# Gated decode attention on one core: V of a step and K of the next as one 8 MiB transfer

## The chip, the core and the metric

The kernel runs on one core of one Trainium2 chip. The metric is device time in microseconds (us) of one execution. TensorE (PE) multiplies matrices, VectorE (DVE) and ScalarE (ACT) work on elements, GpSimd (POOL) does almost nothing here, and SyncE (SP) issues the transfers from the chip's memory. Sixteen DMA engines carry the bytes of this core.

## The reference, cut to what matters

One token for each of two batch entries (B = 2, D = 448) attends to a cache of 4096 positions. There are 16 query heads and 8 key/value heads, each of width 256. All data is fp32. K and V of the cache are 64 MiB each, so that 128 MiB of the 158.54 MB of reads (1 MiB is 1.05 MB) are the cache; the rest is weights.

```python
xn = _layernorm(x)                                   # [2, 1, 448]
q  = (xn @ wq).reshape(B, 1, 16, 256)                # two query heads share one K/V head
scores = einsum("bhqd,bhkd->bhqk", q, k) * 256**-0.5
o  = einsum("bhqk,bhkd->bhqd", softmax(scores), v)
s  = o.reshape(B, 1, 4096) @ wo
h  = (xn @ w_gate) * (xn @ w_up)                     # bilinear GLU
g  = silu(h @ w_down)
return x + s * g
```

## The kernel before

**Steps.** One step is one pair of a K/V head and a batch entry, so there are N = 16 steps, `i` = 0 to 15. Its K and its V are 4 MiB each, laid out in memory as 128 rows of 32 KB, one row for each partition. `scores(i)` (matmuls at L205) multiplies K of the step with the query, `softmax` (L210 to L231) makes the probabilities, and `values(i)` (matmuls at L237) multiplies them with V. `scores` and `values` are 16 matmuls each, which fp32 turns into 32 in the profile. `softmax` is a chain through three engines: a maximum on DVE, a transpose on PE (L213) and a second maximum on DVE that leaves one value in each element of a row, a matmul with a one (L218) that brings this row back to a column, an exponential on ACT, a transpose on DVE, and a matmul (L229) that adds up the sums.

**Work between the steps.** `query(0)` and `query(1)` project the token to queries with `wq0` and `wq1`. `ffn_in` and `ffn_out` compute the gate from `wg`, `wu` and `wd`. `combine` (L246) and `turn` (L256) bring finished outputs into the form that the output projection needs, `project` (L264) does that projection with `wo0` (16 blocks) and `wo1` (8 blocks), `spread` (L167) adds its partial sums up, and `project_last` (L270) does the last 8 blocks, with `wo2`.

**Order.** The instructions of every engine run in the order in which the program writes them (`manual_schedule`). A step of the loop writes `scores(i)`, `softmax`, `values(i)`. After the loop over the first 14 steps come `combine` of 6 outputs, `turn`, `project` with `wo1`, `spread`, then `scores` and `softmax` of step 14, `scores` and `softmax` of step 15, `values(14)`, `values(15)` in two halves, and the small rest.

**Buffers.** All large reads go through one ring of five buffers of 32 KB for each partition. `plan` writes down the order of the reads, `issue` (transfers at L59, all on SP's queue) starts the next ones. SP waits, in order, until the buffer that a transfer needs is free; five transfers are issued before any work. The order is wq0, k0, v0, k1, v1, wg, wu, k2, v2, wd, k3, v3, and so on with one K and one V for each step; its end is k13, v13, wo1, k14, k15, v14, v15 (in three pieces), wo2 (in four pieces). wo1 and wo2 are 1.75 MiB each.

Of the kernel before, what the change touches and what calls it, by code (L numbers as in the profile page):

```python
# [25 lines left out]
EARLY = 16  # L26
LATE = 24
THIRD = [24, 25, 28, 29, 30, 31, 26, 27]
EPS = 1e-5


# [2 lines left out]


@with_exitstack
def gated_decode_block(ctx: ExitStack, tc: tile.TileContext, x, xo, kt, v, wq, wo, wg, wu, wd, out):
    nc = tc.nc
    ring = ctx.enter_context(tc.tile_pool(name="ring", bufs=5))
    const = ctx.enter_context(tc.tile_pool(name="const", bufs=1))  # L40
    work = ctx.enter_context(tc.tile_pool(name="work", bufs=2))
    psum = ctx.enter_context(tc.tile_pool(name="psum", bufs=1, space=bass.MemoryType.PSUM))
# [2 lines left out]
    def bank(name="s", bufs=3):  # L45
        return psum.tile([128, 512], F32, name=name, bufs=bufs)


    loaded = {}
    todo = []  # L50

    def plan(name, src, cuts=None):
        todo.append((name, src, cuts or [0, src.shape[1]]))

    def issue(n=1):
        for name, src, cuts in todo[:n]:
            t = loaded[name] = ring.tile([128, ROW], F32, name="ring", align_bytes=512)
            for lo, hi in zip(cuts, cuts[1:]):
                nc.sync.dma_start(t[:, lo:hi], src[:, lo:hi])  # L59
        del todo[:n]  # L60

    N = HKV * B
    LAST = N - B
    plan("wq0", wq[0])
    for i in range(LAST):
        if i == 2:
            plan("wg", wg)
            plan("wu", wu)
        if i == 3:
            plan("wd", wd)  # L70
        if i == 6:
            plan("wq1", wq[1])
        if i == 9:
            plan("wo0", wo[:, :EARLY * D])
        plan(f"k{i}", kt[i % B, i // B])
        plan(f"v{i}", v[i % B, i // B])
    plan("wo1", wo[:, EARLY * D:LATE * D])
    plan(f"k{LAST}", kt[0, HKV - 1])
    plan(f"k{LAST + 1}", kt[1, HKV - 1])
    plan(f"v{LAST}", v[0, HKV - 1])  # L80
    plan(f"v{LAST + 1}", v[1, HKV - 1], [0, 4096, 7168, 8192])
    plan("wo2", wo[:, LATE * D:], [0, 2 * D, 6 * D, 7 * D, 8 * D])
    issue(5)

    x2 = const.tile([B, D], F32)
    nc.scalar.dma_start(x2, x)
# [48 lines left out]
    def rows(ps, w, n):  # L135


        def block(i):
            return w[:, i * n:(i + 1) * n]

        for k in range(3):
            for c in range(NT):
                nc.tensor.matmul(ps[W * c:W * (c + 1), :n], xnT[:, k, :], block(NT * k + c), start=k == 0, stop=False)  # L143
        for c in range(NT):
            half = slice(0, 64) if c < 2 else slice(64, 128)
            nc.tensor.matmul(ps[W * c:W * (c + 1), :n], xnT[half, 3, :], block(12 + c % 2)[half], start=False, stop=True)  # L146
# [4 lines left out]
    def query(h):  # L151
        ps = bank()
        rows(ps, loaded[f"wq{h}"], 512)
        for r in range(REP):
            nc.vector.transpose(qT[h][:, :, :, :, r, :].rearrange("p b g d j -> p (g d) b j"),  # L155
                                ps[:, r * 256:(r + 1) * 256])
# [10 lines left out]
            nc.tensor.matmul(dst[W * n:W * (n + 1), :SL], add_tiles.rearrange("p b j -> p (b j)"),  # L167
                             t[:, n * SL:(n + 1) * SL], start=start, stop=stop)

    def ffn_in():  # L170
        pp = []
        for w in ("wg", "wu"):
            ps = bank()
            rows(ps, loaded[w], FC)
            pp.append(ps)
        g = work.tile([128, FC], F32, name="h")
        nc.scalar.copy(g, pp[0][:, :FC])
        h = work.tile([128, FC], F32, name="h")
        nc.vector.tensor_mul(h, pp[1][:, :FC], g)
        nc.vector.transpose(hT.rearrange("p i m -> p (i m)"), h)  # L180

    def ffn_out():
        ps = bank()
        for i in range(14):
            t = i % NT
            nc.tensor.matmul(ps[W * t:W * (t + 1), :D], hT[:, i], loaded["wd"][:, i * D:(i + 1) * D],  # L186
                             start=i < NT, stop=i >= 14 - NT)
        y = bank()
        spread(ps, y, True, True)
        e = const.tile([128, SL], F32)  # L190
        nc.scalar.activation(e, y[:, :SL], AF.Sigmoid)
        nc.vector.tensor_mul(gate, y[:, :SL], e)


    def scores(i):
        g, b = divmod(i, B)
        k = loaded[f"k{i}"].rearrange("p (h d c n) -> p h d c n", h=2, d=2, c=NT)
        q = qT[g // 4][:, b, g % 4].rearrange("p d r j -> p d (r j)")
        m = work.tile([128, 4], F32, name="m")
        ss = []  # L200
        for h in range(2):
            s = bank()
            for d in range(2):
                for c in range(NT):
                    nc.tensor.matmul(s[W * c:W * (c + 1), :], q[:, d], k[:, h, d, c, :], start=d == 0, stop=d == 1)  # L205
            nc.vector.tensor_reduce(m[:, h:h + 1], s, axis=AX.X, op=OP.max)  # L206
            ss.append(s)
        return ss, m

    def softmax(ss, m):  # L210
        nc.vector.tensor_max(m[:, 2:3], m[:, 0:1], m[:, 1:2])  # L211
        sm = bank("sm", 1)
        nc.tensor.transpose(sm[:1, :128], m[:, 2:3], ident)  # L213
        mx = work.tile([1, NT, W], F32, name="mx")
        nc.vector.tensor_reduce(  # L215
            mx, sm[:1, None, :128].rearrange("p o (c j) -> p o j c", c=NT).to_broadcast([1, NT, W, NT]),
            axis=AX.X, op=OP.max)
        nc.tensor.matmul(sm[:, 128:129], mx.rearrange("p c j -> p (c j)"), one, start=True, stop=True)  # L218
        nc.vector.tensor_scalar(m[:, 3:4], sm[:, 128:129], -1.0 / 16, None, op0=OP.mult)  # L219
        su = work.tile([128, 4], F32, name="su")  # L220
        pT = []
        for h in range(2):
            p = work.tile([128, 512], F32, name="p")
            nc.scalar.activation(p, ss[h], AF.Exp, bias=m[:, 3:4], scale=1.0 / 16, accum_out=su[:, h:h + 1])  # L224
            t = work.tile([128, KB, W], F32, name="pT", bufs=4)
            nc.vector.transpose(t.rearrange("p i m -> p (i m)"), p)  # L226
            pT.append(t)
        nc.vector.tensor_add(su[:, 2:3], su[:, 0:1], su[:, 1:2])  # L228
        nc.tensor.matmul(sm[:, 130:131], add_head.rearrange("p a r j -> p (a r j)"), su[:, 2:3], start=True, stop=True)  # L229
        nc.vector.reciprocal(su[:, 3:4], sm[:, 130:131])  # L230
        return pT, su[:, 3:4]  # L231

    def values(i, pT, o, lo=0, hi=KB):

        for e in range(lo, hi):
            h, t, at = e // 8, e % NT, e % 8 * 2 * W
            nc.tensor.matmul(o[W * t:W * (t + 1), :], pT[h].rearrange("p i m -> p (i m)")[:, at:at + 2 * W:2],  # L237
                             loaded[f"v{i}"][:, e * 512:(e + 1) * 512], start=e < NT, stop=e >= KB - NT)
# [22 lines left out]
    def project(oT, first, lo, hi, name, base):  # L261
        for i in range(lo, hi):
            t = i % NT
            nc.tensor.matmul(wide[W * t:W * (t + 1), :D], heads(oT, i, first),  # L264
                             loaded[name][:, (i - base) * D:(i - base + 1) * D], start=i < NT, stop=i >= LATE - NT)
# [5 lines left out]
                             start=False, stop=i == THIRD[-1])  # L271

    query(0)
    issue()
    ob = work.tile([128, 8, 512], F32, name="ob", bufs=1)
    oT0 = const.tile([128, 4, 2, REP, W], F32)
    oT1 = const.tile([128, 3, 2, REP, W], F32)
    oT2 = const.tile([128, 1, 2, REP, W], F32)
    for i in range(LAST):
        g, b = divmod(i, B)  # L280
        ss = scores(i)
        issue()
        p = softmax(*ss)
        o = bank("o", 1)
        values(i, p[0], o)
        nc.scalar.activation(ob[:, b * 4 + g if g < 4 else b * 3 + g - 4], o, AF.Copy, scale=p[1])  # L286
        issue()
        if i == 1:
            ffn_in()
            issue(2)  # L290
        if i == 2:
            ffn_out()
            issue()
        if i == 5:
            query(1)
            issue()
        if i == 7:
            cb = combine(ob, 8)
            for n in range(B):
                turn(oT0, cb[:, n * 256:(n + 1) * 256], 0, n, 4)  # L300
            ob = work.tile([128, 8, 512], F32, name="ob", bufs=1)
        if i == 8:
            project(oT0, 0, 0, EARLY, "wo0", 0)
            issue()
    cb = combine(ob, 6)
    for n in range(B):
        turn(oT1, cb[:, n * 192:(n + 1) * 192], 0, n, 3)
    project(oT1, 4, EARLY, LATE, "wo1", EARLY)
    issue()
    spread(wide, acc, True, False)  # L310
    ps = []
    for i in range(LAST, N):
        ss = scores(i)
        issue()
        ps.append(softmax(*ss))

    o = bank("o", 1)
    values(LAST, ps[0][0], o)
    nc.scalar.activation(ob[:, 6], o, AF.Copy, scale=ps[0][1])
    issue()  # L320
    o = bank("wide", 1)
    values(LAST + 1, ps[1][0], o, 0, KB // 2)
    cb = combine(ob[:, 6:], 1)
# [55 lines left out]
```

## Time and profile before

| | |
|---|---|
| median of 3 runs | 378.04 us (377.98 to 378.4) |
| the profiled execution, time | 378.55 us |
| its span | 376.4 us |
| bytes read | 158.54 MB |
| PE busy | 222.5 us (59%) |
| DVE busy | 72.7 us (19%) |
| ACT busy | 39.8 us (11%) |
| mean granted TensorE clock | 0.772 |

The span runs from the first to the last instruction of the profiled execution; 2.15 us of its time lie outside it. "PE" is a matmul row, "PEld" the load of the operand that stays in the array. A row of the timeline gives start, length, engine, line, operation and, in brackets, the idle time before it and who ended it. One transfer appears on SP with the length of its issue, and where somebody waits for its landing, as "DMA" with the buffer and the source.

### The profile page before, as it was taken

To read this page: it belongs to the slowest core of one execution; us is meant where nothing else is said; L and a number is where in the kernel's file an instruction comes from. 1 tells how busy PE (TensorE), PEld (TensorE's weight loads), DVE (VectorE), ACT (ScalarE), POOL (GpSimd) and SP (SyncE) were. 2 spreads that over 40 slices of the span, in tenths; PEclk is the share of its full clock that TensorE was granted. 3 is DMA by queue.
4 is the path that set the end of the run, shared out by engine and by line. 5 is a ranking of instruction groups with operands and counts; after the bars stand their busy time and mean duration, and the time that the engine had idled before them with its cause. 6 is when DMAs were issued, how large, how long until landed. Compare 5 with 4: busy or idle time off the path is not lost.

```text
span 376.4 us, 3397 instructions
## 1 busy us (share of the span) xinstructions
PE 222.5 (59%) x1456; PEld 65.6 (17%) x1456; DVE 72.7 (19%) x176; ACT 39.8 (11%) x87; POOL 1.2 (0%) x7
## 2 busy tenths in 40 slices
PE   0665556566376566646566655664656475574775
PEld 0112111112122111101121111121112121111122
DVE  3013030121021402102121310222112210304211
ACT  1001011001202200200102110011101010111011
POOL 1000000000000000000000000000000000000000
PEclk9966869766965877687886978669686966699669
DMA  8999999999999999999999999999999999999993
GB/s 333 437 439 416 435 430 438 428 429 444 425 434 439 435 420 436 438 435 432 420 439 437 432 424 432 442 437 421 427 442 435 435 423 428 435 428 445 414 417 132
DMA packets 6530, 158.75 MB, mean 422 GB/s; under 512 B 754, under 2 KB 1012, under 8 KB 1396
## 3 DMA queue, kind: packets, MB, share of 16 engines
q1 hardware_dynamic: 6496, 158.54, 98.0%
q8 instruction: 11, 0.18, 0.2%
q14 instruction: 3, 0.02, 0.0%
q10 hardware_dynamic: 20, 0.01, 0.0%
HBM read 158.54 MB, written 0.00 MB: 421 GB/s over the span
## 4 chain that ended last, share of the span: by engine, by line
DMA 76%; PE 18%; DVE 3%; issue 1%; ACT 1%; SPq 0%; ACTq 0%
DMA ring<-kt 55%; DMA ring<-v 12%; DMA ring<-wd 9%; PE s L205 8%; PE o L237 6%; DVE pT L226 1%; PE wide L237 1%; PE s L186 1%; PE cb L246 1%; DVE m L206 1%; DVE mx L215 1%; PE sm L229 0%; PE acc L270 0%; SPq L59 0%; PE sm L218 0%
## 5 line engine op out<-in xcount | busy, mean ns | idle before, releaser
L205 PE MATMUL s<-ring,qT 128*32 128x512 f32 x512 | 82.0, 799 | 50.9 <-DMA ring<-kt 50.9
L237 PE MATMUL o<-ring,pT 128*32 128x512 f32 x480 | 82.4, 849 | 1.6 <-DMA ring<-v 1.6
L206 DVE TENSOR_REDUCE m<-s 128x1 f32<-128x512 f32 x32 | 22.1, 692 | 177.5 <-PE s L205 177.5
L224 ACT ACTIVATE p<-s,m 128x512 f32<-128x512 f32 x32 | 21.7, 682 | 197.1 <-DVE m L219 197.1
L205 PEld LDWEIGHTS s<-ring,qT 128*32 128x32 f32 x512 | 20.5, 141 | 110.3 <-issue 78.5
L229 PE MATMUL sm<-su,add_head 128*128 128x1 f32 x32 | 9.4, 362 | 42.4 <-DVE su L228 42.4
L237 PEld LDWEIGHTS o<-ring,pT 128*32 128x32 f32 x480 | 18.9, 149 | 51.5 <-issue 50.9
L226 DVE STREAM_TRANSPOSE pT<-p 128x512 f32<-128x512 f32 x32 | 22.1, 711 | 15.7 <-ACT p L224 15.7
L143 PE MATMUL s<-ring,xnT 128*32 128x512 f32 (+1 forms) x96 | 14.3, 746 | 12.3 <-DMA ring<-wq 7.7
L286 ACT ACTIVATE ob<-o,su 128x512 f32<-128x512 f32 x14 | 9.6, 687 | 98.8 <-PE o L237 98.8
L229 PEld LDWEIGHTS sm<-su,add_head 128*128 128x128 f32 x32 | 8.0, 311 | 43.8 <-DVE su L228 43.8
L213 PE MATMUL sm<-ident,m 128*1 128x128 f32 x16 | 4.3, 270 | 17.3 <-DVE m L211 17.3
L218 PE MATMUL sm<-one,mx 1*128 1x1 f32 x32 | 6.8, 279 | 12.3 <-DVE mx L215 12.3
L215 DVE TENSOR_REDUCE mx<-sm 1x128 f32<-1x512 f32 x16 | 10.9, 679 | 7.0 <-PE sm L213 7.0
L264 PE MATMUL wide<-ring,oT 128*32 128x448 f32 x48 | 6.6, 698 | 4.1 <-DMA ring<-wo 3.3
L218 PEld LDWEIGHTS sm<-one,mx 1*128 1x128 f32 x32 | 5.4, 211 | 15.8 <-DVE mx L215 15.8
L143 PEld LDWEIGHTS s<-ring,xnT 128*32 128x32 f32 x96 | 3.6, 132 | 21.0 <-issue 17.0
L213 PEld LDWEIGHTS sm<-ident,m 128*1 128x1 f32 x16 | 1.3, 79 | 32.4 <-issue 26.6
L256 DVE STREAM_TRANSPOSE oT<-cb 128x256 f32<-128x256 f32 (+2 forms) x6 | 1.9, 347 | 25.5 <-PE cb L246 25.5
L224 ACT ACTIVATION_READ_ACCUMULATOR p<-s,m 128x1 f32 x32 | 6.3, 196 | 0.0
L155 DVE STREAM_TRANSPOSE qT<-s 128x256 f32<-128x256 f32 x4 | 1.6, 428 | 21.6 <-PE s L146 21.6
L246 PE MATMUL cb<-ob,add_blocks 128*32 128x64 f32 (+2 forms) x64 | 4.2, 384 | 2.3 <-ACT ob L286 1.6
(57 smaller groups left out, 47.0 us busy)
## 6 DMA issues: line engine op xcount, KB each, us to landing
ring<-kt SPq DMA_DIRECT2D x16, 4096.0 KB, 40.4
ring<-v SPq DMA_DIRECT2D x15, 4096.0 KB, 41.8
ring<-wq SPq DMA_DIRECT2D x2, 3584.0 KB, 11.3
ring<-wo SPq DMA_DIRECT2D x1, 3584.0 KB, 40.7
ring<-wg SPq DMA_DIRECT2D x1, 3136.0 KB
ring<-wu SPq DMA_DIRECT2D x1, 3136.0 KB
ring<-wd SPq DMA_DIRECT2D x1, 3136.0 KB, 34.5
ring<-v SPq DMA_DIRECT2D x1, 2048.0 KB
```

Source lines behind the costliest of these rows:

```text
L143: nc.tensor.matmul(ps[W * c:W * (c + 1), :n], xnT[:, k, :], block(NT * k + c), start=k == 0, stop=False)
L205: nc.tensor.matmul(s[W * c:W * (c + 1), :], q[:, d], k[:, h, d, c, :], start=d == 0, stop=d == 1)
L206: nc.vector.tensor_reduce(m[:, h:h + 1], s, axis=AX.X, op=OP.max)
L215: nc.vector.tensor_reduce(mx, sm[:1, None, :128].rearrange("p o (c j) -> p o j c", c=NT).to_broadcast([1, NT, W, NT]), axis=AX.X, op=OP.max)
L218: nc.tensor.matmul(sm[:, 128:129], mx.rearrange("p c j -> p (c j)"), one, start=True, stop=True)
L224: nc.scalar.activation(p, ss[h], AF.Exp, bias=m[:, 3:4], scale=1.0 / 16, accum_out=su[:, h:h + 1])
L226: nc.vector.transpose(t.rearrange("p i m -> p (i m)"), p)
L229: nc.tensor.matmul(sm[:, 130:131], add_head.rearrange("p a r j -> p (a r j)"), su[:, 2:3], start=True, stop=True)
L237: nc.tensor.matmul(o[W * t:W * (t + 1), :], pT[h].rearrange("p i m -> p (i m)")[:, at:at + 2 * W:2], loaded[f"v{i}"][:, e * 512:(e + 1) * ...
L246: nc.tensor.matmul(cb[W * c:W * (c + 1), :n * 64], add_blocks[:, e].rearrange("p r j -> p (r j)"), src[:, :n, e, :, c, :], start=e == 0, s ...
L264: nc.tensor.matmul(wide[W * t:W * (t + 1), :D], heads(oT, i, first), loaded[name][:, (i - base) * D:(i - base + 1) * D], start=i < NT, sto ...
L286: nc.scalar.activation(ob[:, b * 4 + g if g < 4 else b * 3 + g - 4], o, AF.Copy, scale=p[1])
```

## The change

The host writes V of step i and K of step i + 1 side by side, so that a row of this block is 64 KB; 14 such blocks of 8 MiB are one transfer each. k0 and v15 stay single, and k15 and v14 share a buffer but come as two transfers. The ring has two buffers of 64 KB instead of five of 32 KB, and all weights go through one buffer of 28 KB of their own (`slot`). The order of the reads is wq0, k0, [v0 k1], wg, [v1 k2], wu, [v2 k3], wd, [v3 k4], [v4 k5], wq1, and so on up to [v12 k13], wo1, [v13 k14], k15, v14, v15, wo2. Three transfers are issued before any work instead of five.

The program order follows: `scores(0)` and its `softmax` stand ahead of the loop, and step i of the loop writes `values(i)`, `scores(i + 1)`, the issue of what comes next, and `softmax` of step i + 1; then the work with weights, if the step has any. So `scores(14)` and its `softmax` stand in the last pass of the loop, ahead of `combine` of the 6 outputs. `ffn_in` is split into `gate_in` (after softmax of step 1) and `up_in` (after that of step 2). In `softmax`, the matmul with a one at L218 becomes a transpose, with the same operands.

```diff
-    ring = ctx.enter_context(tc.tile_pool(name="ring", bufs=5))
+    ring = ctx.enter_context(tc.tile_pool(name="ring", bufs=2))
+    slot = ctx.enter_context(tc.tile_pool(name="slot", bufs=1))
...
-            t = loaded[name] = ring.tile([128, ROW], F32, name="ring", align_bytes=512)
+            if len(names) == 1 and names[0].startswith("w"):
+                t = loaded[names[0]] = slot.tile([128, PART], F32, name="slot", align_bytes=512)
+            else:
+                t = ring.tile([128, 2 * ROW], F32, name="ring", align_bytes=512)
+                for i, name in enumerate(names):
+                    loaded[name] = t[:, i * ROW:(i + 1) * ROW]
...
+    plan("k0", first)
+    weights = {0: ("wg", wg), 1: ("wu", wu), 2: ("wd", wd), 4: ("wq1", wq[1]), 8: ("wo0", wo[:, :EARLY * D]),
+               12: ("wo1", wo[:, EARLY * D:LATE * D])}
     for i in range(LAST):
...
-        plan(f"k{i}", kt[i % B, i // B])
-        plan(f"v{i}", v[i % B, i // B])
...
+        plan(f"v{i} k{i + 1}", vk[i])
+        if i in weights:
+            plan(*weights[i])
+    plan(f"k{LAST + 1} v{LAST}", last0, [0, ROW, 2 * ROW])
+    plan(f"v{LAST + 1}", last1, [0, 4096, 7168, 8192])
     plan("wo2", wo[:, LATE * D:], [0, 2 * D, 6 * D, 7 * D, 8 * D])
-    issue(5)
+    issue(3)
...
-        nc.tensor.matmul(sm[:, 128:129], mx.rearrange("p c j -> p (c j)"), one, start=True, stop=True)
+        nc.tensor.transpose(sm[:, 128:129], mx.rearrange("p c j -> p (c j)"), one)
...
     query(0)
-    issue()
...
+    ss = scores(0)
+    issue(2)
+    p = softmax(*ss)
     for i in range(LAST):
         g, b = divmod(i, B)
-        ss = scores(i)
-        issue()
-        p = softmax(*ss)
         o = bank("o", 1)
         values(i, p[0], o)
+        ss = scores(i + 1)
+
+        n, late = 1 + (i + 1 in weights), i in weights and i + 1 in weights
+        if not late:
+            issue(n)
         nc.scalar.activation(ob[:, b * 4 + g if g < 4 else b * 3 + g - 4], o, AF.Copy, scale=p[1])
-        issue()
...
+        p = softmax(*ss)
...
+        if i == LAST - 1:
+            cb = combine(ob, 6)
+            for n in range(B):
+                turn(oT1, cb[:, n * 192:(n + 1) * 192], 0, n, 3)
+        if i in weights:
...
+        if late:
+            issue(n)
     project(oT1, 4, EARLY, LATE, "wo1", EARLY)
     issue()
     spread(wide, acc, True, False)
-    ps = []
-    for i in range(LAST, N):
-        ss = scores(i)
-        issue()
-        ps.append(softmax(*ss))
+    ps = [p]
+    ss = scores(LAST + 1)
+    ps.append(softmax(*ss))
```

More of the change, by code (lines that the diff above doesn't have):

```diff
@@ L28, with gated_decode_block @@
 THIRD = [24, 25, 28, 29, 30, 31, 26, 27]
+PART = EARLY * D
 EPS = 1e-5
 @with_exitstack
-def gated_decode_block(ctx: ExitStack, tc: tile.TileContext, x, xo, kt, v, wq, wo, wg, wu, wd, out):
+def gated_decode_block(ctx: ExitStack, tc: tile.TileContext, x, xo, first, vk, last0, last1, wq, wo, wg, wu, wd, out):
     nc = tc.nc
-    ring = ctx.enter_context(tc.tile_pool(name="ring", bufs=5))
+    ring = ctx.enter_context(tc.tile_pool(name="ring", bufs=2))
+    slot = ctx.enter_context(tc.tile_pool(name="slot", bufs=1))
     const = ctx.enter_context(tc.tile_pool(name="const", bufs=1))
@@ L46, in bank @@
         return psum.tile([128, 512], F32, name=name, bufs=bufs)
+    N = HKV * B
+    LAST = N - B
     loaded = {}
     todo = []
-    def plan(name, src, cuts=None):
-        todo.append((name, src, cuts or [0, src.shape[1]]))
     def issue(n=1):
-        for name, src, cuts in todo[:n]:
-            t = loaded[name] = ring.tile([128, ROW], F32, name="ring", align_bytes=512)
+        for names, src, cuts in todo[:n]:
+            if len(names) == 1 and names[0].startswith("w"):
[4 more added lines that the diff above has]
+                    loaded[name] = t[:, i * ROW:(i + 1) * ROW]
             for lo, hi in zip(cuts, cuts[1:]):
@@ L60, in issue, with plan @@
         del todo[:n]
-    N = HKV * B
-    LAST = N - B
+    def plan(names, src, cuts=None):
+        todo.append((names.split(), src, cuts or [0, src.shape[1]]))
     plan("wq0", wq[0])
+    plan("k0", first)
+    weights = {0: ("wg", wg), 1: ("wu", wu), 2: ("wd", wd), 4: ("wq1", wq[1]), 8: ("wo0", wo[:, :EARLY * D]),
+               12: ("wo1", wo[:, EARLY * D:LATE * D])}
     for i in range(LAST):
[L66 to L74, printed above, removed]
-        plan(f"k{i}", kt[i % B, i // B])
-        plan(f"v{i}", v[i % B, i // B])
[L77 to L81, printed above, removed]
+        plan(f"v{i} k{i + 1}", vk[i])
[3 more added lines that the diff above has]
+    plan(f"v{LAST + 1}", last1, [0, 4096, 7168, 8192])
     plan("wo2", wo[:, LATE * D:], [0, 2 * D, 6 * D, 7 * D, 8 * D])
-    issue(5)
+    issue(3)
     x2 = const.tile([B, D], F32)
@@ L168, in spread, with gate_in, up_in @@
                              t[:, n * SL:(n + 1) * SL], start=start, stop=stop)
[L170 to L177, printed above, removed]
+    def gate_in():
+        ps = bank()
+        rows(ps, loaded["wg"], FC)
+        g = const.tile([128, FC], F32)
+        nc.scalar.copy(g, ps[:, :FC])
+        return g
+    def up_in(g):
+        ps = bank()
+        rows(ps, loaded["wu"], FC)
         h = work.tile([128, FC], F32, name="h")
-        nc.vector.tensor_mul(h, pp[1][:, :FC], g)
+        nc.vector.tensor_mul(h, ps[:, :FC], g)
         nc.vector.transpose(hT.rearrange("p i m -> p (i m)"), h)
@@ L278, in gated_decode_block @@
     oT2 = const.tile([128, 1, 2, REP, W], F32)
+    ss = scores(0)
+    issue(2)
+    p = softmax(*ss)
     for i in range(LAST):
         g, b = divmod(i, B)
-        ss = scores(i)
-        issue()
-        p = softmax(*ss)
         o = bank("o", 1)
         values(i, p[0], o)
+        ss = scores(i + 1)
+        n, late = 1 + (i + 1 in weights), i in weights and i + 1 in weights
+        if not late:
+            issue(n)
         nc.scalar.activation(ob[:, b * 4 + g if g < 4 else b * 3 + g - 4], o, AF.Copy, scale=p[1])
-        issue()
[L288 to L292, printed above, removed]
-            issue()
-        if i == 5:
-            query(1)
-            issue()
+        p = softmax(*ss)
         if i == 7:
@@ L301, in gated_decode_block @@
             ob = work.tile([128, 8, 512], F32, name="ob", bufs=1)
[L302 to L307, printed above, removed]
+        if i == LAST - 1:
[3 more added lines that the diff above has]
+        if i in weights:
+            if i == 0:
+                gt = gate_in()
+            if i == 1:
+                up_in(gt)
+            if i == 2:
+                ffn_out()
+            if i == 4:
+                query(1)
+            if i == 8:
+                project(oT0, 0, 0, EARLY, "wo0", 0)
+        if late:
+            issue(n)
     project(oT1, 4, EARLY, LATE, "wo1", EARLY)
@@ L310, in gated_decode_block @@
     spread(wide, acc, True, False)
-    ps = []
-    for i in range(LAST, N):
-        ss = scores(i)
-        issue()
-        ps.append(softmax(*ss))
+    ps = [p]
+    ss = scores(LAST + 1)
+    ps.append(softmax(*ss))
     o = bank("o", 1)
@@ L319, in gated_decode_block @@
     nc.scalar.activation(ob[:, 6], o, AF.Copy, scale=ps[0][1])
-    issue()
     o = bank("wide", 1)
@@ L352 @@
     k = np.asarray(A_k_cache).reshape(B, HKV, NT, W, 2, KB, 2, 128)
-    kt = c(k.transpose(0, 1, 7, 4, 6, 2, 5, 3)).reshape(B, HKV, 128, ROW)
-    v = c(A_v_cache).reshape(B, HKV, 128, ROW)
+    k = k.transpose(1, 0, 7, 4, 6, 2, 5, 3).reshape(HKV * B, 128, ROW)
+    v = np.asarray(A_v_cache).reshape(B, HKV, 128, ROW).transpose(1, 0, 2, 3).reshape(HKV * B, 128, ROW)
+    n = HKV * B - B
+    first = c(k[0])
+    vk = np.concatenate([v[:n], k[1:n + 1]], 2)
+    last = [np.concatenate([k[n + 1], v[n]], 1), c(v[n + 1])]
     def folded(w, n):
@@ L370 @@
     nc = bacc.Bacc("TRN2", target_bir_lowering=False, num_devices=1, dynamic_dma_scratch_size=2048)
-    arrays = dict(x=x, xo=xo, kt=kt, v=v, wq=wq, wo=wo, wg=wg, wu=wu, wd=wd)
+    arrays = dict(x=x, xo=xo, first=first, vk=vk, last0=last[0], last1=last[1], wq=wq, wo=wo, wg=wg, wu=wu, wd=wd)
     args = [nc.dram_tensor(n, a.shape, mybir.dt.from_np(a.dtype), kind="ExternalInput").ap()
```

## The prediction, on record before the changed kernel had run

> **What bounds the kernel now.** I read the page's slices and queue rows first, then the windows of the end, then PE's timeline there.
>
> ```profile
> DMA  8999999999999999999999999999999999999993
> q1 hardware_dynamic: 6496, 158.54, 98.0%
> ```
>
> The 16 DMA engines are busy in every slice but the first and the last, 98.0% of the span on SP's queue. Up to the last reads the kernel is as fast as its stream: 0.98 × 376.4 = 368.9 us of packets. No wait of an engine in the middle is worth anything by itself. The end is different:
>
> ```profile
> 360.00:370.00 10.00, 9.57 (x86) 3.04 (x90) 0.80 (x4) 0.69 (x1) 0.00 (x0) 0.76 0.94 393
> 370.00:376.40 6.40, 2.33 (x84) 1.60 (x76) 0.80 (x3) 0.69 (x1) 0.00 (x0) 0.90 0.08 28
> ```
>
> (Columns: window, its length, busy us and instructions of PE, PEld, DVE, ACT, POOL, the granted clock, the DMA share, GB/s.) From 360 us on PE is busy nearly without a gap, while the stream ends near 370. So PE sets the end, and the question is where this PE chain starts. PE's timeline before it:
>
> ```profile
> 327.41 5.26 PE L237 MATMUL o<-ring,pT 128*32 128x512 f32 x32
> 333.49 1.50 PE L246 MATMUL cb<-ob,add_blocks 128*32 128x384 f32 x16 [0.82 <-ACT ob L286]
> 335.75 1.71 PE L264 MATMUL wide<-ring,oT 128*32 128x448 f32 x16 [0.77 <-DVE oT L256]
> 338.11 0.40 PE L167 MATMUL acc<-h,add_tiles 128*32 128x112 f32 x8 [0.65 <-ACT h L165]
> 339.19 3.64 PE L205 MATMUL s<-ring,qT 128*32 128x512 f32 x32 [0.67 <-DMA ring<-kt]
> ...
> 347.92 0.58 PE L229 MATMUL sm<-su,add_head 128*128 128x1 f32 x2 [2.57 <-DVE su L228]
> 348.84 6.49 PE L205 MATMUL s<-ring,qT 128*32 128x512 f32 x32 [0.34 <-DMA ring<-kt]
> ...
> 360.43 0.58 PE L229 MATMUL sm<-su,add_head 128*128 128x1 f32 x2 [2.58 <-DVE su L228]
> ```
>
> This is the row of most weight. `values(13)` runs at 327.41, long before k14 lands (339.1, where `scores(14)` ends its idle time on "DMA ring<-kt"). `combine`, `project` and `spread` fill the stretch up to that landing with 0.67 us to spare. `scores(14)` and its softmax then end 0.34 us before k15 lands (348.8). Everything is done just in time; `values(14)` starts at 360.95, and from there 376.4 − 360.95 = 15.45 us remain.
>
> **The stream, changed.** The bytes are the same, and so is what must have arrived before k14 is complete: all but k15, v14, v15 and wo2. So [v13 k14] lands when k14 did, at 339.1, if the stream has the same rate and never runs dry.
>
> Rate: in the trace's packet records a 32 KB row takes 1214 ns and a 16 KB row 611, which is 9 ns and 27.2 bytes per ns; the packet that signals an engine's end of a transfer also takes 9. Each of 14 blocks has 8 rows per engine, so 112 row overheads and 14 signals fall away: 126 × 9 ns = 1.1 us. If a 64 KB row is still cut into two packets, only 0.1 us is saved. Nothing before shows a row over 32 KB, so it could also be lost (a rival below). I take −0.7.
>
> Running dry: two buffers mean that the next block is issued only when a block has been used. A block lands, `values(i)` (5.0 to 6.5 us) and `scores(i+1)` run back to back, and the buffer is free. Such a pair stands in the trace already:
>
> ```profile
> 116.63 6.54 PE L237 MATMUL o<-ring,pT 128*32 128x512 f32 x32
> 123.00 3.61 PE L205 MATMUL s<-ring,qT 128*32 128x512 f32 x32
> ```
>
> That is 10.0 us from start to end; the second runs at the full clock because the first has warmed PE (3.6 instead of 5.0 to 6.5 after a pause; the granted clock is 0.96 in the window 330 to 340 us, where PE has no long pause, and 0.67 in 350 to 360). The other block streams for 8.39 MB / 432 GB/s = 19.4 us, so SP has some 9 us to spare. In steps 0 and 1 the issue stands behind the softmax (5.7 us, 342.83 to 348.50) and the work with a weight (3.4 to 5.1 us, the rows of `ffn_in`), at 18 to 21 us; but there a weight of 3.2 MB is queued too, and the engines have 26.9 us of work. The first three transfers hold 16.3 MB, 37 us, and the next issue waits only for `scores(0)`, some 28 us in. SP has nothing else queued behind these waits. The stream stays full; the smaller number of issues (0.33 us each on SP) is hidden as well.
>
> **The end, changed.** Here the program order costs. `values(13)` can no longer run at 327.41, since v13 lands together with k14 at 339.1; and `combine`, `project` and `spread`, which used the wait for k14, now stand behind the softmax of step 14 on PE, ahead of `scores(15)`. PE's chain from 339.2 on:
>
> - `values(13)` and `scores(14)`: 7.3 us warm (2 × 3.64), 10.0 in the pair above, whose first part was cold throughout. First parts after a pause take 5.0 to 6.5, so 8.7 to 10.2; I take 9.4.
> - softmax(14) up to the end of its L229: 5.67 (342.83 to 348.50). PE has only three small instructions here and must wait inside each; nothing behind them can pass.
> - `combine` to the end of `spread`, with the hops over DVE and ACT: 333.49 to 338.51 = 5.0 at the full clock. `scores(15)` at the full clock: 3.64. PE comes out of a softmax, after which the rows show slow starts (5.0 to 6.5 instead of 3.64, so 1.4 to 2.9 lost). I add 2.1 once for both, for 10.8 together; 8.7 with nothing lost, 12 with a long slow stretch.
> - softmax(15) up to `values(14)`: 355.33 to 360.95 = 5.62.
>
> Sum: 9.4 + 5.67 + 10.8 + 5.62 = 31.5, so `values(14)` starts at 339.2 + 31.5 = 370.7 instead of 360.95: +9.7 us. k15 lands at 348.8 and v14, v15 and wo2 by about 372, all before PE asks, so the 15.45 us behind it stay. The time moves from waits for transfers to PE, and the stream idles at the end.
>
> **The transpose at L218.** fp32 matmuls appear twice (x32 for 16 calls), the transpose at L213 once. The pair takes 0.38 to 0.58, the single one 0.27: some 0.12 less in each softmax, of which two lie on the chain: −0.25 (0 to −0.6). In the other 14 the stream hides it. Splitting `ffn_in` costs nothing where it stands, for the same reason.
>
> **Sum.** +9.7 − 0.25 − 0.7 = +8.75. The profiled execution (378.55, 2.15 of it outside the span) would become 387.3, with a span of 385.15; the median of the runs was 378.04, so I predict 386.8. Bounds of the terms: the chain 28.7 to 33.5 (+6.9 to +11.7), small terms −1.7 to 0, so 383.3 to 389.7.
>
> **Rivals.**
> - *Faster, or the same: the long rows raise the stream's rate.* The place is the 14 blocks, 117.4 MB. From 430 GB/s to the best slice of the page, 445, they would take 263.9 us instead of 273.1: 9.2 us earlier. With the chain above that is 378.3, no change; with PE warm all along (7.3 + 5.67 + 8.7 + 5.62, +5.4) it is 374.0. It decides from about 440 GB/s on as a mean. Against it, 16 engines at 27.2 bytes per ns make 435, and the windows already show 434 and 436. Chances: 0.04 faster, 0.02 the same. The Trainium skill ("DMA: Bandwidth & Descriptors", Anatomy of one DMA) gives a fixed 2.0 us for each transfer on another issue path; paid in series for 14 transfers fewer it would take 28 us off, an estimate of 358.8. The trace speaks against a serial cost, with 98.0% of the span in packets.
> - *Slower than forecast: 64 KB rows stream worse.* At the page's worst middle slice, 414 GB/s, the blocks take 283.6, +10.5; the end follows, 397 to 398. The rows of 24.5, 28 and 32 KB take 0.93, 1.09 and 1.21 us, in step with their size, with no sign of it. Chance 0.05. The Trainium skill's rule in "DMA: Bandwidth & Descriptors", Latency and other measured facts, speaks against the change: rows at a large power-of-two pitch in memory slow a copy (207 of 214 GB/s at 512 KiB). No run so far has a 64 KB pitch; by that ratio 3.3% of 273 us, an estimate of +9 us, would come on top.
> - *Slower than forecast: the stream runs dry at each block.* It decides if a buffer is freed later than 19.4 us after its landing; then each block costs the issue and the start of the first bytes (issue at 0.74 us, first packet near 1.76) and its lateness: 14 × 1.4 = 19 us, 406. The pair of 10.0 us speaks against it. Chance 0.03.
>
> **How the numbers follow.** The forecast has 0.86. Its bounds, stretched by 0 to 2 us for an end whose clock windows fall otherwise, give 383.5 to 391.5. What this kernel's measurement can tell from no change is about 0.2%, 0.8 us. Faster 0.04, the same 0.02, slower 0.86 + 0.05 + 0.03 = 0.94.
>
> **What would show it.** Right: the slices stay full up to about 370 us; [v13 k14] lands near 338 to 339; then two L237/L205 groups back to back, a softmax, `combine`, `project`, `spread`, `scores(15)` without one wait for DMA; `values(14)` starts near 370; the last slices of DMA are empty. The rows of the blocks take about 2.42 us if uncut. Wrong: 442 GB/s in the middle slices, or 3s and 5s among the 9s of the DMA row, or a wait for DMA on the last chain.

## The result and the profile after

The changed kernel takes 387.66 us, median of 6 runs (385.99 to 388.03); the kernel before, beside it, 378.22 (377.97 to 378.8). The ratio is 1.0237, 95% interval 1.0214 to 1.0261: slower, by 9.4 us from median to median. The profiled execution is one of the shorter ones, 386.21 us with a span of 384.1, against 376.4 before.

First the page's slices and queue row of the changed kernel:

```profile
DMA  8999998999999999999999999999999999999940
q1 hardware_dynamic: 4480, 158.54, 95.8%
```

The same bytes fill the same stretch; what is new is the 4 and the 0 at the end (the 8 in the seventh slice comes from how packets are counted, see the rivals below). The stream did not grow, it stopped and the core went on: the packet records of the queue add up to 367.8 us for each engine (95.8% of 384.1), before to 368.8 (98.0% of 376.4). The two windows at the end say it in numbers (columns as above):

```profile
360.00:370.00 10.00, 5.55 (x40) 1.83 (x36) 3.97 (x9) 1.45 (x4) 0.00 (x0) 0.80 0.90 373
370.00:384.10 14.10, 9.83 (x152) 3.64 (x144) 1.05 (x4) 1.37 (x2) 0.00 (x0) 0.86 0.02 6
```

In the last 14.1 us almost nothing is read (6 GB/s) and PE works. In the packet records of the two traces the last piece of wo2 ends at 371.5 us, before at 372.3; the span ends 12.6 us behind it, before 4.1. PE's timeline of the end:

```profile
338.50 5.43 PE L239 MATMUL o<-ring,pT 128*32 128x512 f32 x32 [10.01 <-DMA ring<-vk]
343.74 3.62 PE L207 MATMUL s<-ring,qT 128*32 128x512 f32 x32
...
352.29 0.52 PE L231 MATMUL sm<-su,add_head 128*128 128x1 f32 x2 [2.57 <-DVE su L230]
352.74 2.79 PE L248 MATMUL cb<-ob,add_blocks 128*32 128x384 f32 x16
356.29 1.71 PE L266 MATMUL wide<-slot,oT 128*32 128x448 f32 x16 [0.77 <-DVE oT L258]
358.65 0.40 PE L167 MATMUL acc<-h,add_tiles 128*32 128x112 f32 x8 [0.65 <-ACT h L165]
358.87 3.62 PE L207 MATMUL s<-ring,qT 128*32 128x512 f32 x32
...
367.42 0.58 PE L231 MATMUL sm<-su,add_head 128*128 128x1 f32 x2 [2.58 <-DVE su L230]
367.94 6.06 PE L239 MATMUL o<-ring,pT 128*32 128x512 f32 x32
```

(L239, L207, L231, L248 and L266 are the old L237, L205, L229, L246 and L264.) The first row has the reading of most weight: PE sits idle for 10.01 us, until the whole block [v13 k14] has landed, and then `values(13)` and `scores(14)` run back to back. From there on no row waits for a transfer. `values(13)`, which began at 327.41 before, begins at 338.50, and `combine`, `project` and `spread` stand between the softmax of step 14 and `scores(15)`. `values(14)` starts at 367.94 instead of 360.95.

### The profile page after: what moved, and what is told of

It reads as the page before. It is cut to its first block, busy times and chain, and to the rows that moved or that the text cites. A ratio compares the mean times of both kernels' runs of the same rounds, so it can differ in the third digit from the quotient of the medians.

```text
span 384.1 us, 3333 instructions
## 1 busy us (share of the span) xinstructions
PE 204.3 (53%) x1440; PEld 61.5 (16%) x1440; DVE 72.7 (19%) x176; ACT 39.8 (10%) x87; POOL 1.2 (0%) x7
## 3 DMA queue, kind: packets, MB, share of 16 engines
q1 hardware_dynamic: 4480, 158.54, 95.8%
## 4 chain that ended last, share of the span: by engine, by line
DMA 69%; PE 25%; DVE 3%; issue 1%; ACT 1%; SPq 0%; ACTq 0%
DMA ring<-vk 64%; PE o L239 12%; PE s L207 9%; DMA ring<-first 5%; DVE pT L228 1%; PE s L143 1%; PE wide L239 1%; PE cb L248 1%; DVE m L208 1%; DVE mx L217 1%; PE wide L266 0%; PE sm L231 0%; PE acc L272 0%; PE s L146 0%; DVE oT L258 0%
## 5 line engine op out<-in xcount | busy, mean ns | idle before, releaser
L239 PE MATMUL o<-ring,pT 128*32 128x512 f32 x480 | 84.9, 872 | 86.7 <-DMA ring<-vk 86.7
L207 PE MATMUL s<-ring,qT 128*32 128x512 f32 x512 | 59.4, 605 | 3.1 <-DMA ring<-first 3.1
L239 PEld LDWEIGHTS o<-ring,pT 128*32 128x32 f32 x480 | 20.9, 153 | 142.4 <-issue 126.8
L231 PE MATMUL sm<-su,add_head 128*128 128x1 f32 x32 | 8.7, 340 | 42.4 <-DVE su L230 42.4
L207 PEld LDWEIGHTS s<-ring,qT 128*32 128x32 f32 x512 | 17.3, 112 | 42.4 <-issue 38.6
L143 PE MATMUL s<-slot,xnT 128*32 128x512 f32 (+1 forms) x96 | 18.1, 916 | 5.7 <-DMA slot<-wq 5.7
L231 PEld LDWEIGHTS sm<-su,add_head 128*128 128x128 f32 x32 | 7.3, 284 | 43.8 <-DVE su L230 43.8
L220 PE MATMUL sm<-one,mx 1*128 1x1 f32 x16 | 3.5, 221 | 12.4 <-DVE mx L217 12.4
L248 PE MATMUL cb<-ob,add_blocks 128*32 128x64 f32 (+2 forms) x64 | 7.2, 586 | 0.6 <-ACT ob L331 0.6
L266 PE MATMUL wide<-slot,oT 128*32 128x448 f32 x48 | 6.4, 679 | 0.8 <-DVE oT L258 0.8
L143 PEld LDWEIGHTS s<-slot,xnT 128*32 128x32 f32 x96 | 4.1, 160 | 15.2 <-issue 15.2
L215 PEld LDWEIGHTS sm<-ident,m 128*1 128x1 f32 x16 | 1.3, 79 | 31.5 <-issue 27.7
L188 PE MATMUL s<-slot,hT 128*32 128x448 f32 x28 | 4.8, 799 | 0.0
```

Of the source, the lines that this page charges most:

```text
L248: nc.tensor.matmul(cb[W * c:W * (c + 1), :n * 64], add_blocks[:, e].rearrange("p r j -> p (r j)"), src[:, :n, e, :, c, :], start=e == 0, s ...
```

## The experiments

Three theories were set against each other. **The end:** v13 lands together with k14, so that work which used the wait for k14 now lies behind it. **The stream:** two buffers or 64 KB rows make the reads slower. **The order:** the changed program order of the end is the cause by itself.

**Cut one block.** Only [v13 k14] comes as two transfers, into the same buffer.

```diff
-        plan(f"v{i} k{i + 1}", vk[i])
+        plan(f"v{i} k{i + 1}", vk[i], [0, ROW, 2 * ROW] if i == LAST - 1 else None)
```

> The changed kernel, with one block only, [v13 k14], issued as two transfers of 4 MiB into the same buffer; program order as changed. Theory (the end): v13 lands some 9.7 us earlier, values(13) runs before k14 lands, and the pair of 8.9 us behind the landing shrinks to scores(14) alone, 3.6 to 6.5 us by the clock. The rest of the chain stays: 2.4 to 5.2 us less than 387.7, so 382.5 to 385.3. Rival (the stream is worse with two buffers or 64 KB rows): 387.7, no change. Rival (the program order, combine and project behind the softmax of step 14, is the cause by itself): 387 or more.

Measured: 382.7 us (380.59 to 384.65), ratio 1.0108 (1.0078 to 1.0139). PE's timeline:

```profile
328.98 4.97 PE L239 MATMUL o<-ring,pT 128*32 128x512 f32 x32 [0.83 <-DMA ring<-vk]
338.54 5.31 PE L207 MATMUL s<-ring,qT 128*32 128x512 f32 x32 [4.59 <-DMA ring<-vk]
```

`values(13)` starts 9.5 us earlier than in the changed kernel, though still 1.6 later than before (327.41), and 5 us are gone with one cut in one transfer; the other 13 blocks, the buffers and the order are untouched. Part of what is won goes back to the clock: `scores(14)` now starts after a pause and takes 5.31 instead of 3.62 us.

**Cut one block and put the order back.**

```diff
         values(i, p[0], o)
-        ss = scores(i + 1)
+        if i < LAST - 1:
+            ss = scores(i + 1)
...
     project(oT1, 4, EARLY, LATE, "wo1", EARLY)
-    issue()
     spread(wide, acc, True, False)
-    ps = [p]
+    ss = scores(LAST)
+    issue(2)
+    ps = [softmax(*ss)]
```

(The issue and the softmax of the last pass of the loop are left out there in the same way.)

> As the run with the cut last block, and the end in the order of the kernel before: values(13), combine, turn, project, spread, scores(14), softmax, scores(15), softmax. Theory (the end): all of +9.7 goes; values(14) starts where it did in the kernel before, less 0.7 of the stream and 0.2 to 0.5 of the transposes: 377.0 to 377.8, so a little under the kernel before. Rival (the stream): stays over 385, since the other 13 blocks, the two buffers and the 64 KB rows are as in the changed kernel.

Measured: 378.07 us (377.65 to 379.8), ratio 1.0000 (0.9987 to 1.0012). The whole loss is gone while both buffers and the 64 KB rows of 13 blocks stay, so the stream is not the cause. With v13 landing early, the program order is worth 4.6 us (from 382.7 to 378.07). The expectation that this kernel would come out a little under the kernel before missed. PE's timeline of the profiled execution, at 377.66 one of the shortest:

```profile
327.86 0.59 PE L231 MATMUL sm<-su,add_head 128*128 128x1 f32 x2 [2.57 <-DVE su L230]
328.38 5.45 PE L239 MATMUL o<-ring,pT 128*32 128x512 f32 x32
...
339.50 3.62 PE L207 MATMUL s<-ring,qT 128*32 128x512 f32 x32
...
370.45 1.56 PE L272 MATMUL acc<-slot,oT 128*32 128x112 f32 x48 [0.63 <-DMA slot<-wo]
```

`values(13)` starts at 328.38, 1 us later than before, and `scores(14)` at 339.50, without waiting, behind `spread`. And the last group of matmuls now waits 0.63 us for wo2: in this execution the end of the stream itself holds the kernel. The second set of runs below shows that this is not so in each.

**Only put the order back**, with all blocks whole; the edit is the second one above alone.

> The changed kernel with all 14 blocks whole, and only the program order of the end put back: values(13), combine, turn, project, spread, scores(14), softmax, scores(15), softmax. Theory (the end): the same work lies behind the same landing; 5.4 + 0.8 + 5.0 + 0.7 + 3.6 + 5.5 + (3.6 to 6.5) + 5.5 = 30.1 to 33.0 instead of 29.4, so 388 to 391, no gain. Rival (program order alone is the cause): 378. Rival (the stream): 387.7.

Measured: 386.51 us (386.05 to 388.42), ratio 1.0223 (1.0203 to 1.0244).

```profile
338.41 5.18 PE L239 MATMUL o<-ring,pT 128*32 128x512 f32 x32 [10.45 <-DMA ring<-vk]
...
369.14 5.18 PE L239 MATMUL o<-ring,pT 128*32 128x512 f32 x32
```

The order alone brings back almost nothing (the runs of the changed kernel reach from 385.99 to 388.03), so it is not the cause without the landing. The number lies below the expected 388 to 391: the chain was 30.7 us (338.41 to 369.14) against 29.4 in the changed kernel, as expected, but `values(14)` and what follows took 15.3 us instead of 16.2, at a granted clock of 0.92 from 370 us on instead of 0.86.

**The loss without the change.** In the kernel before, v13 is read behind k14, so that it lands when k14 did.

```diff
-        plan(f"v{i}", v[i % B, i // B])
+        if i < LAST - 1:
+            plan(f"v{i}", v[i % B, i // B])
     plan("wo1", wo[:, EARLY * D:LATE * D])
     plan(f"k{LAST}", kt[0, HKV - 1])
+    plan(f"v{LAST - 1}", v[(LAST - 1) % B, (LAST - 1) // B])
```

> The kernel before, five buffers and rows of 32 KB, with one edit: V of step 13 is read behind K of step 14, so that it lands when K of step 14 used to land, at 339.1 us. Theory (the end): values(13), combine, project, spread, scores(14), softmax, scores(15), softmax all lie behind 339.1: 5.4 + 0.8 + 5.0 + 0.7 + 3.6 + 5.7 + (3.6 to 6.5) + 5.6 = 30.4 to 33.3 instead of 21.8, so 387 to 389.5, the slowdown of the change without its stream. Rival (the stream): 378.2, since rate, rows and buffers are those of the kernel before. Rival (program order alone): 378.2, since it is unchanged.

Measured: 387.85 us (386.88 to 389.04), ratio 1.0258 (1.024 to 1.0276).

```profile
338.66 5.24 PE L239 MATMUL o<-ring,pT 128*32 128x512 f32 x32 [12.84 <-DMA ring<-v]
```

Five buffers, 32 KB rows and the old program order lose as much as the change did, once v13 lands at 338.7. So the landing of v13 beside k14 is enough for the loss by itself; with v13 early, as the runs above show, the changed order still costs about half of it.

**Cut all blocks**, beside the kernel with one cut and the old order, on the same chip.

```diff
-        plan(f"v{i} k{i + 1}", vk[i], [0, ROW, 2 * ROW] if i == LAST - 1 else None)
+        plan(f"v{i} k{i + 1}", vk[i], [0, ROW, 2 * ROW])
```

> The kernel with the last block cut and the end in the order of before, once more, as the partner of the next runs on the same chip: 377.0 to 377.8.

> As its partner, with all 14 blocks issued as two transfers of 4 MiB with rows of 32 KB. Theory (each packet costs 9 ns beside its bytes): 13 blocks x 8 rows per engine and 13 signals more, 117 x 9 ns = 1.05 us later than the partner. Rival (long rows stream worse): 1 us or more earlier than the partner. Rival (long rows raise the rate): several us later.

Measured: the partner 378.14 us (377.66 to 379.41), ratio 1.0003 (0.9992 to 1.0015), again above what was expected; all cut 378.42 (377.96 to 379.61), ratio 1.0008 (0.9997 to 1.0019). The packets of the queue take 368.88 us for each engine instead of 367.75: 1.1, where 1.05 was worked out. In the time 0.3 us show, which the intervals can't tell from nothing. Two rows of the partner (378.15 in its profiled execution) and then one of the kernel with all blocks cut show what else holds these kernels:

```profile
328.88 5.87 PE L239 MATMUL o<-ring,pT 128*32 128x512 f32 x32 [1.34 <-DMA ring<-vk]
...
371.14 1.36 PE L272 MATMUL acc<-slot,oT 128*32 128x112 f32 x48 [0.18 <-DVE oT L258]
```

```profile
329.02 5.15 PE L239 MATMUL o<-ring,pT 128*32 128x512 f32 x32 [3.14 <-DMA ring<-vk]
```

v13 itself lands only near 329 us, even with all blocks cut, where PE waits 3.14 us for it. The order of the reads fits this: the changed kernel reads wo1 ahead of v13, the kernel before read it behind. No run put wo1 back, so this is not shown. And in the partner's profile the last group does not wait for wo2, whose last piece ends at 371.5 us: there PE's chain sets the end, and the stream ends about as late.

**The transpose alone**, in the kernel before.

```diff
-        nc.tensor.matmul(sm[:, 128:129], mx.rearrange("p c j -> p (c j)"), one, start=True, stop=True)
+        nc.tensor.transpose(sm[:, 128:129], mx.rearrange("p c j -> p (c j)"), one)
```

> The kernel before with only the maximum's return (L218) as a transpose. Theory: one pass instead of two in each softmax; the two softmaxes of the last chain save 0.12 to 0.25 each, so 0.25 to 0.5 us in all: 377.7 to 378.0. The other 14 are hidden by the stream. Rival (a transpose costs as much): no change.

Measured: 378.16 us (377.8 to 378.37), ratio 0.9998 (0.999 to 1.0007): no difference that can be measured, where 0.25 to 0.5 us less was expected. The step itself is shorter (0.22 us instead of 0.38), but in the profiled execution the last group waits for the stream:

```profile
355.99 0.22 PE L218 MATMUL sm<-one,mx 1*128 1x1 f32 x1 [0.77 <-DVE mx L215]
...
371.19 1.16 PE L270 MATMUL acc<-ring,oT 128*32 128x112 f32 x40 [0.83 <-DMA ring<-wo]
```

**Keep PE warm.** Five matmuls that nobody reads, in the waits of the last two softmaxes: one ahead of the first transpose, four behind the second.

```diff
+        if fill is not None:
+            for _ in range(4):
+                nc.tensor.matmul(idle[:, :256], add_head.rearrange("p a r j -> p (a r j)"), fill, start=True, stop=True)
```

(The four behind the second transpose are shown; the one ahead of the first is the same call.)

> The kernel with the last block cut and the end in the order of before, and five extra matmuls of 256 columns, whose result nobody reads, in the waits of each of the last two softmaxes. Theory (the granted clock falls in the softmax's waits and makes scores(15) 6.5 instead of 3.6 us and values(14) 5.6 instead of 3.6): values(14) starts 2.5 to 3 us earlier and takes 2 us less; V of step 15, which lands near 368, then sets the end: 1 to 2 us under its partner, about 375.5. Rival (the extra matmuls delay the softmax's own PE steps as much as they save): the same as its partner or up to 3 us more.

> The changed kernel as it is, with the five extra matmuls of 256 columns, whose result nobody reads, in the softmaxes of steps 14 and 15 only. It sizes the clock's part of the chain. Theory (the chain on PE sets the end, and part of it is run at half the clock after each softmax): combine falls from 2.8 to 1.5 us and values(14) from 6.1 to 3.6, with scores(15) at 3.6 as it was: 3.7 us less than the changed kernel's profile of 386.2, so 382.5, and the runs lie closer together than 386.0 to 388.0. Rival (the clock plays no part, only the order): 386 to 388.

Measured, on the kernel with one cut and the old order: 377.68 us (377.48 to 378.47), ratio 0.999 (0.9981 to 0.9998); on the changed kernel as it is: 381.74 (381.25 to 383.01), ratio 1.0097 (1.0076 to 1.0117). Rows of PE's timeline, first of the changed kernel with the extra matmuls, then of the other:

```profile
352.50 1.50 PE L254 MATMUL cb<-ob,add_blocks 128*32 128x384 f32 x16
...
366.12 3.64 PE L245 MATMUL o<-ring,pT 128*32 128x512 f32 x32
```

```profile
349.66 3.64 PE L207 MATMUL s<-ring,qT 128*32 128x512 f32 x32
...
362.53 1.92 PE L245 MATMUL wide<-ring,pT 128*32 128x512 f32 x16 [0.43 <-DMA ring<-last]
...
366.19 2.27 PE L245 MATMUL wide<-ring,pT 128*32 128x512 f32 x16 [1.51 <-DMA ring<-last]
...
370.78 1.39 PE L278 MATMUL acc<-slot,oT 128*32 128x112 f32 x48 [0.91 <-DMA slot<-wo]
```

In the changed kernel `combine` falls from 2.79 to 1.50 us and `values(14)` from 6.06 to 3.64, with a granted clock of 1.00 in the three windows from 345 to 375 us, where the changed kernel had 0.80 to 0.89 in its windows from 340 us on. The time falls by 5.9 us from median to median, and by 4.3 between the two profiled executions (386.21 and 381.94): where PE's chain sets the end, the clock does too. (The runs lie hardly closer together than those of the changed kernel; that part of the expectation missed.) In the other kernel the windows from 340 to 370 us also show a granted clock of 1.00, and `values(14)` starts 2.1 us earlier than in its partner's profile (358.46 and 360.54). But PE now waits for v15 (1.51 us) and wo2 (0.91), so that the landing of a piece of wo2 at 370.8 and 4.9 us of work behind it set the end. That is why the expected 1 to 2 us under the partner did not come; this is the fastest of the kernels, but 0.1% is less than what a measurement of this kernel can tell from no change.

## Why the prediction was right

387.66 us were measured, 386.8 predicted. The mechanism is the one that was forecast; its steps, each against the profiled execution:

- **The stream keeps its rate and never runs dry.** Shown. In every microsecond from 3 to 367 more than 15 of the 16 engines on average are inside a packet. A 64 KB row is one packet of 2418 ns in the packet records, which is 9 ns and 27.2 bytes per ns, so the forecast's fit holds beyond the sizes it came from. The Trainium skill's rule on rows at a large power-of-two pitch ("DMA: Bandwidth & Descriptors", Latency and other measured facts) had given an estimate of 9 us more; at a pitch of 64 KB the trace shows nothing of it, since 2418 ns is less than twice the 1213 of a 32 KB row. SP issued the next block 9 to 10 us after a landing (179.4 us for a block that landed at 169.6, in the chain of waits), or, in steps 0 and 1, 19 to 20 us (60.9 for 40.97), in time each time.
- **The landing, 0.7 earlier.** The packets are 1.0 us shorter for each engine, near the 1.1 worked out. The block lands at 338.5 (339.2 before), but this one difference is not safe: the same landing came at 338.41 and 338.01 in other executions with whole blocks, and at 338.66 with the 32 KB rows of the kernel before.
- **The chain.** 9.4, 5.67, 10.8 and 5.62 were taken; the rows give 8.86 (338.50 to 347.36), 5.38, 9.75 (352.74 to 362.49) and 5.45: 29.4. The forecast had 31.5, or 31.25 with the transposes, which were a term of their own. The largest part of the difference is the slow start behind the softmax: `combine` took 2.79 us instead of 1.50, and `scores(15)` was not slowed, so 1.3 us were lost where 2.1 were taken. The transpose at L220 saves about 0.2 in each softmax, the upper half of what was given for it.
- **The 15.45 us behind `values(14)` stay.** Not quite: 16.16, since `values(14)` met a slow stretch (6.06 instead of 5.56).
- **The rivals.** Faster by long rows: the packets won 1.0 us for each engine, not 9.2. Single slices of the new page reach 491 and 477 GB/s, over the 442 that was named as a sign of this; but others stand at 378 and 388. A slice counts a packet where it starts, and these take 2.4 us: spread over the packets' own time, no slice from the second to the 37th lies above 434 GB/s (433 before). Worse by long rows, or a dry stream: excluded by the run with one cut and the old order, at 378.07 with the same buffers and, in 13 blocks, the same rows. (The chain with PE warm all along adds up to +5.5, not the +5.4 given; nothing hangs on it.)

That the number came within 1 us is in part luck. The span of the profiled execution was 384.1 instead of 385.15: a chain 1.8 us too long and a tail 0.7 too short cancel in part, +7.7 us where +8.75 was forecast. The medians have +9.4. Of the runs of the changed kernel, 385.99 and 386.21 had a mean granted clock of 0.781 and 0.777, the four from 387.5 to 388.03 had 0.733 to 0.751, and none of these four was traced.

What the prediction had not seen is how close the stream and PE's chain end in the kernel before, where it says that PE sets the end. Its profile bears this out (the last group waits 0.18 us for DVE), but with only the transpose added the last group already waited 0.83 us for wo2. So even with the end repaired, the stream's 0.7 us and the transposes' 0.4 us could hardly show. Nor did it see that v13, read behind wo1, would land near 329 us even as a transfer of its own, when `values(13)` had started at 327.41 before.

## What to carry to other kernels

Work that waits for a joined transfer waits for all of it: here `values(13)` started at 338.50 with the block whole and at 328.98 with the block cut in two. In the middle of a full stream that cost nothing that could be measured (378.14 with 13 blocks whole, 378.42 with all cut); at its end, read PE's timeline from the last landings on and add up what lies behind each. Before making transfers longer, fit time against row size in the packet records: 9 ns for each row of 1.2 us was all that could be won. And when the end of the stream already holds the kernel, shorter steps ahead of it show nothing.

## What the runs showed of the hardware that was not expected

After the idle stretches of a softmax (1.1, 0.8 and 2.6 us in the rows), the next group of 16 matmuls took 5.0 to 6.5 us instead of 3.6. Ten matmul instructions of 0.7 and 2.0 us together, put into the waits of each of the last two softmaxes, held the granted clock at 1.00 and took 5.9 us off the changed kernel. The same filling in a kernel whose stream ends about as late as PE was worth 0.5 us at most. Nor was it expected that the changed kernel would move by 2 us from one execution to the next, along with its granted clock; the kernel before moved by 0.8 us beside it, and by 1.5 over all its 35 runs beside the later kernels. The mean clock does not explain every such difference: with one block cut, executions at a clock of 0.755 took 380.6 and 380.7 us, and one at 0.792 took 382.8. Why they differ is not known.
